# Row maxima ahead of attention placed a little sooner behind DVE by the clock of the program

## The chip, the cores and the metric

The kernel runs on one core of a Trainium2 chip. The metric is the device time of one execution in microseconds; of the kernel before, three runs took 1078.60, 1079.80 and 1075.82 us, with a median of 1078.6 us. The engines are named as in the profile: PE multiplies matrices (PEld is its weight load, which overlaps with the multiplication), DVE and POOL do elementwise work and reductions, ACT does activations and copies, and SP, ACT and POOL issue DMAs. PE writes into PSUM, which has eight banks here (`bk`, 128 partitions x 8 banks x 512 floats).

## The reference

One input x of 2048 tokens by 448 features goes through two branches, and a gate per token mixes them.

```python
qkv = (x @ wqkv).reshape(B, S, 3, H, Dh)          # H = 16 heads, Dh = 28
scores = einsum("bhqd,bhkd->bhqk", q, k) * (Dh ** -0.5)
p = softmax(scores, axis=-1)
a = einsum("bhqk,bhkd->bhqd", p, v) ... @ wo      # branch a: attention
y = layernorm(x)
h = gelu(y @ w1 + b1)                             # 448 -> 1792
b = h @ w2 + b2                                   # branch b: an MLP, 1792 -> 448
g = sigmoid((x * gate_w).sum(-1))
out = g * a + (1 - g) * b
```

The softmax needs, for each head and each query, the largest score over the 2048 keys. The kernel finds it ahead of the attention by computing the scores once more in a cheaper form, and that work is what the change touches.

## The kernel before

**Tiling.** The 2048 tokens are four chunks of 512. The 16 heads are four groups of four, and a group's heads sit in four bands of 32 partitions, so that four matmuls with 28 to 32 contraction rows can work side by side, one in each band of PE's rows. A matmul of the projections or of the MLP is cut into such bands too ("strips"): each strip works through its quarter of the contraction and hands the accumulating bank to the next strip. Values that need more than one pass of the fast float format are split in a high and a low part (`xh`/`xl`, `yh`/`yl`, `w2h`/`w2l`, `hh`/`hl`, `khi`/`klo`).

**Stages.** First come the projections `QK` (query and key, written to DRAM as `qk`) and `Val` (values). Then, per chunk, come 14 `Up` tiles (448 to 1792, weights `w1f`) and 4 `Down` tiles (1792 to 448). All these are pieces of the class `Strips`. Then comes attention, in "turns": a turn computes scores for 5, 6 or 7 units (a unit is 128 keys x 512 queries of one head, three matmuls of line 1179 into one bank), takes their exponentials on ACT (line 1183), and multiplies earlier exponentials with the values (line 1192, a batch is the four heads of one key block). There are 1024 units and 256 batches.

**Row maxima.** There are also 1024 steps of a row maximum. A step (`RowMax.one`, lines 212 and 214) is one matmul of 128 queries x 512 keys (`qd`, `kd`) into a bank and one DVE reduction of that bank to 128 numbers (`mx`). During `Strips` two banks, 6 and 7, serve the steps in turn, so that a step's matmul cannot start before the reduction of the step before last has read the same bank. When a block of 64 steps is complete, DVE reduces it further and transposes it (`close`), SP stores it in DRAM, and the attention loads it as an extra row of the queries.

**What sets the order of PE's instructions.** The order is written out ahead by `Strips.run`, which keeps a clock of its own for each of the four strips and for DVE, ACT and POOL, all from constants in the code. A strip whose clock is lowest is asked first for a row maximum (`Strips.rowmax`), and if it has none, for the next matmul of a piece. If neither can be had, its clock moves on by 0.1 us. A row maximum is given only when its bank's entry in the table `rm` is not later than the strip's clock. That entry is set to the planned end of the bank's reduction plus a pause; a reduction is planned with 0.65 us (`RM`). The clocks decide nothing on the chip. There, engines go through their instructions in the order written, and wait on semaphores.

**What is left over goes into attention.** Steps that `Strips.run` has not placed by its end are placed by `lone` inside the turns of the attention. A turn of 5 units has room for three of them, a turn of 6 for two. `turn_of` makes a turn of 5 as long as more steps are left than the coming turns of 6 could take:

```python
size = 5 if owed and owed > 2 * ((left - 104) // 6) + 6 * sixes[0] else 6
```

Here `owed` is the number of steps left and `left` the number of units left. Turns of 7 come only when no step is left.

Of the kernel before, what the change touches and what calls it, by code (L numbers as in the profile page):

```python
# [35 lines left out]
def kernel(ctx: ExitStack, tc: tile.TileContext, xt, wqk, wv, wo, xk, w1, b1, w2, b2,  # L36
# [367 lines left out]
    class Strips:  # L404
# [92 lines left out]
        def rowmax(self, s, now):  # L497
            if now < self.hot[s] or not rowmax.ready(s):
                return False
            if rowmax.cnt[s] > 5 + min(rowmax.cnt):  # L500
                return False
            b = min(self.rm, key=lambda b: self.rm[b])
            if self.rm[b] > now:
                return False
            ends = rowmax.one(s, bk[:, b])
            self.t[s] = now + 0.232
            self.use("dve", now + 0.45, RM)
            self.rm[b] = self.dve + 0.1
            for kind, n, j in ends:
                if kind == "q":  # L510
                    self.at(now + 6.0, lambda n=n, j=j: rowmax.load_q(n, j))
                elif kind == "k":
                    def load(n=n, j=j):
                        rowmax.load_k(n, j)
                        self.hot[j] = self.get(self.clock + 0.6, 224) + 1.0

                    self.at(now + 1.5, load)
                    self.hot[j] = 1e9
                else:
                    self.at(now + 0.5, lambda n=n: rowmax.close(n), dve=0.45)  # L520
                    self.at(now + 3.0, lambda n=n: rowmax.store(n))
            return True
# [678 lines left out]
    while b < UNITS // 4:  # L1201
# [13 lines left out]
        while 4 * b + 4 <= before and quota:  # L1215
# [7 lines left out]
            b, begun_half = b + 1, False  # L1223
# [59 lines left out]
```

## Time and profile before

The profiled execution took 1078.01 us, with a span of 1076.2 us from its first to its last instruction and a granted TensorE clock of 1.000. It is 0.6 us shorter than the median of the runs.

| what | value |
|---|---|
| median of three runs | 1078.6 us |
| profiled execution / its span | 1078.01 / 1076.2 us |
| row maximum: reduction on DVE (line 214) | x1024, 673.8 us, mean 688 ns |
| row maximum: matmul on PE (line 212) | x1024, 449.4 us busy, mean 440 ns |
| exponentials on ACT (line 1183) | x381, 481.0 us, mean 1316 ns |
| first matmul with `w1f` (start of the MLP) | 125.2 us |
| first score matmul of attention (line 1179) | 450.0 us |

Times count from the start of the span. A busy time of PE is a union of overlapping matmuls, each of which shows about 0.4 us although several run side by side in the four bands, so PE looks full nearly throughout. The busy times of PEld, DVE and ACT say more of what is full in a stage. A row of the timeline gives the start, the time covered, the engine, the line, the operation with its tiles, and how many instructions are merged in it. In brackets stand the idle time of the engine before it and what ended that.

### The profile page before, as it was taken

How to read it: one execution, taken by the hardware profiler on the slowest of the kernel's cores; microseconds unless marked ns; L12 is line 12 of the kernel's file. 1: busy time of each engine (PE TensorE's matmuls, PEld its weight loads, DVE VectorE, ACT ScalarE, POOL GpSimd, SP SyncE). 2: the span in 40 equal slices, each digit the busy share in tenths (PEclk: the TensorE clock that was granted, in tenths of full speed). 3: DMA queues.
4: the chain of work that ended last, by engine and by line, in shares of the span. 5: the costliest groups of instructions: out<-in, count | busy, mean ns of one | idle time of the engine just before them, and what ended most of it. 6: DMA issues, size and time to landing. Idle time of an engine off the chain costs nothing.

```text
span 1076.2 us, 31074 instructions
## 1 busy us (share of the span) xinstructions
PE 1065.3 (99%) x13442; PEld 725.8 (67%) x13442; DVE 740.3 (69%) x1201; ACT 633.2 (59%) x654; POOL 367.5 (34%) x388
## 2 busy tenths in 40 slices
PE   9999999999999999999999999999999999999997
PEld 7999999999999999844444444444444444464555
DVE  4899898999999999876767655676764444422102
ACT  5234364033133033288788788778888888857671
POOL 4565578336244037341001101300110315444431
PEclk9999999999999999999999999999999999999999
DMA  7696433312100104230000001210001201011111
GB/s 252 198 285 196 173 105 95 96 46 61 46 7 7 46 14 116 90 80 18 24 12 27 16 24 46 78 42 6 26 25 27 68 23 55 25 59 31 62 49 66
DMA packets 47785, 73.20 MB, mean 68 GB/s; under 512 B 13840, under 2 KB 28816, under 8 KB 46848
## 3 DMA queue, kind: packets, MB, share of 16 engines
q1 hardware_dynamic: 33888, 39.11, 12.0%
q0 software_dynamic: 5120, 16.89, 5.7%
q10 hardware_dynamic: 8640, 15.21, 3.9%
q8 instruction: 105, 1.72, 0.6%
q14 instruction: 32, 0.26, 0.1%
HBM read 51.75 MB, written 19.31 MB: 66 GB/s over the span
## 4 chain that ended last, share of the span: by engine, by line
PE 97%; ACT 1%; issue 1%; DMA 0%; DVE 0%; DVEq 0%; SPq 0%; ACTq 0%
PE bk L488 35%; PE bk L1192 22%; PE bk L1179 19%; PE bk L212 15%; PE bk L1004 1%; ACT p L1183 1%; PE bk L1005 1%; PE bk L1006 1%; PE bk L920 1%; DMA first<-in_xt 0%; PE bk L948 0%; DVE acc L1011 0%; PE bk L905 0%; PE bk L1079 0%; PE bk L1073 0%
## 5 line engine op out<-in xcount | busy, mean ns | idle before, releaser
L214 DVE TENSOR_REDUCE mx<-bk 128x1 f32<-128x512 f32 x1024 | 673.8, 688 | 215.8 <-PE bk L212 173.3
L1183 ACT ACTIVATE p<-bk 128x1536 f32<-128x1536 f32 (+1 forms) x381 | 481.0, 1316 | 122.5 <-PE bk L1179 122.5
L212 PE MATMUL bk<-kd,qd 28*128 28x512 f32 x1024 | 449.4, 440 | 0.1
L212 PEld LDWEIGHTS bk<-kd,qd 28*128 28x128 f32 x1024 | 186.0, 182 | 176.6 <-DVE mx L214 117.2
L488 PE MATMUL bk<-yh,w1f 32*128 32x512 f32 x1568 | 191.6, 393 | 0.0
L488 PE MATMUL bk<-yl,w1f 32*128 32x512 f32 x784 | 166.6, 391 | 0.0
L488 PEld LDWEIGHTS bk<-yh,w1f 32*128 32x128 f32 x1568 | 154.7, 183 | 1.1
L488 PE MATMUL bk<-w2h,hh 32*128 32x448 f32 x896 | 145.6, 367 | 0.2 <-issue 0.2
L488 PE MATMUL bk<-w2l,hh 32*128 32x448 f32 x896 | 144.5, 363 | 0.0
L1192 PE MATMUL bk<-p,va 128*32 128x512 f32 (+1 forms) x1136 | 130.0, 559 | 0.0
L1192 PE MATMUL bk<-p,vb 128*32 128x512 f32 (+1 forms) x1184 | 129.4, 542 | 0.0
L363 POOL TENSOR_TENSOR hl<-h,hh 128x512 fp32r<-128x512 f32 x56 | 72.5, 1307 | 135.0 <-ACT hh L356 111.7
L840 POOL CAST yh<-yl 128x512 fp32r<-128x512 f32 x16 | 9.8, 611 | 314.7 <-DMA yl<-qk 188.0
L488 PEld LDWEIGHTS bk<-yl,w1f 32*128 32x128 f32 x784 | 106.0, 183 | 0.1
L488 PEld LDWEIGHTS bk<-w2h,hh 32*128 32x128 f32 x896 | 103.1, 183 | 0.9 <-issue 0.6
L488 PEld LDWEIGHTS bk<-w2l,hh 32*128 32x128 f32 x896 | 103.1, 183 | 0.3
L1179 PE MATMUL bk<-yh,ka 29*128 29x512 f32 x512 | 100.6, 483 | 0.4 <-ACT p L1183 0.4
L1179 PE MATMUL bk<-yh,kb 29*128 29x512 f32 x512 | 95.9, 480 | 1.6 <-ACT p L1183 1.6
L488 PE MATMUL bk<-w2h,hl 32*128 32x448 f32 x896 | 93.5, 362 | 0.0
L1179 PE MATMUL bk<-yh,la 28*128 28x512 f32 x512 | 82.9, 393 | 0.0
L488 PEld LDWEIGHTS bk<-w2h,hl 32*128 32x128 f32 x896 | 82.2, 183 | 0.3
L1179 PE MATMUL bk<-yl,ka 28*128 28x512 f32 x512 | 81.8, 407 | 0.0
(142 smaller groups left out, 1528.5 us busy)
## 6 DMA issues: line engine op xcount, KB each, us to landing
qk<-qo ACTq DMA_DIRECT2D x28, 256.0 KB
raw<-in_xt SPq DMA_DIRECT2D x17, 256.0 KB
vs<-vt ACTq DMA_DIRECT2D x16, 256.0 KB
rc<-rls SPq DMA_DIRECT2D x60, 64.0 KB
bxr<-in_xk POOLq DMA_DIRECT2D x8, 448.0 KB, 5.9
acc<-gbs SPq DMA_DIRECT2D x16, 224.0 KB
out_y<-acc SPq DMA_DIRECT2D x16, 224.0 KB
qd<-qk SPq DMA_DIRECT2D x60, 56.0 KB
```

The lines of the kernel that those rows point to most:

```text
L212: nc.tensor.matmul(ps, self.qd[n % 2][r, i * P:(i + 1) * P], self.kd[r, k * 512:(k + 1) * 512], start=True, stop=True)
L214: nc.vector.reduce_max(self.mx[n % 2][:, j, i, k:k + 1], ps, axis=AX)
L363: nc.gpsimd.tensor_sub(hl[f], h, hh[f].bitcast(F32))
L488: mm = nc.tensor.matmul(bk[:, x.bank, :n], a, b, start=x.first, stop=(len(x.rem) == 1 and m == len(ops) - 1), skip_group_check=True)
L840: nc.gpsimd.tensor_copy(h, l.bitcast(F32))
L920: nc.tensor.matmul(bk[:, b], w, v, start=(i == 0), stop=(i == len(ops) - 1), skip_group_check=True)
L1004: nc.tensor.matmul(po, h, woh[:, g], start=(g == 0), stop=False, skip_group_check=True)
L1005: nc.tensor.matmul(po, h, wol[:, g], start=False, stop=False, skip_group_check=True)
L1006: nc.tensor.matmul(po, l, woh[:, g], start=False, stop=(g == NG - 1), skip_group_check=True)
L1179: nc.tensor.matmul(bk[:, place(i)], w[r, ks], q[r], start=(p == 0), stop=(p == 2), skip_group_check=True)
L1183: nc.scalar.activation(t[:, :count], bk[:, b:b + count], AF.Exp, scale=SCALE)
L1192: nc.tensor.matmul(bk[32 * j:32 * j + 32, 7, sl], vg[n // NC][:, k, 32 * j:32 * j + 32], prob[4 * b + j][:, sl], start=(k == 0), stop=(k = ...
```

## The change

One constant in `Strips.rowmax` becomes smaller: the pause between the planned end of a bank's reduction and the moment from which that bank may be given to the next row maximum.

```diff
@@ Strips.rowmax
             ends = rowmax.one(s, bk[:, b])
             self.t[s] = now + 0.232
             self.use("dve", now + 0.45, RM)
-            self.rm[b] = self.dve + 0.1
+            self.rm[b] = self.dve + 0.05
             for kind, n, j in ends:
```

No instruction's work changes, and no tile, bank, load or semaphore is added or removed. What changes is the order of the matmuls on PE from the first stage on, with what follows from it on DVE, ACT, POOL and SP, and how many row maxima stand ahead of the attention. Counted in PE's order, 6762 strip matmuls of line 488 stand ahead of the first score matmul in both kernels. Of the row maxima (line 212) 116 stand ahead of the first matmul with `w1f` in both; ahead of the first score matmul stand 578 before and 571 now, so that 446 before and 453 now are left to the attention. The attention had 124 turns of 5 units, 59 of 6, 7 of 7, one of 1 and a last one of none. Now it has 133 of 5, 51 of 6, 7 of 7, one of 4 and a last one of none: 193 turns instead of 192.

The first place is DVE's order around the end of the strips and the start of attention. It begins behind the third of the three gate instructions (lines 849 to 851, issued when the last `Up` tile is done), and ends at the first copy of an attention result (line 1027). `mx` are row maxima; lines 229 and 230 close a block. The kernel before:

```order
L214 TENSOR_REDUCE mx_154<-bk 128x1 x41
L214 TENSOR_REDUCE mx_155<-bk 128x1 x4
L214 TENSOR_REDUCE mx_154<-bk 128x1 x4
L214 TENSOR_REDUCE mx_155<-bk 128x1
L214 TENSOR_REDUCE mx_154<-bk 128x1
L214 TENSOR_REDUCE mx_155<-bk 128x1 x3
L229 TENSOR_REDUCE mf_156<-mx_154 128x16
L230 STREAM_TRANSPOSE mt_158<-mf_156 128x32
L214 TENSOR_REDUCE mx_155<-bk 128x1 x33
L1027 COPY ob<-bk 128x256
```

The changed kernel at the same place on DVE:

```order
L214 TENSOR_REDUCE mx_154<-bk 128x1 x46
L214 TENSOR_REDUCE mx_155<-bk 128x1
L214 TENSOR_REDUCE mx_154<-bk 128x1 x2
L214 TENSOR_REDUCE mx_155<-bk 128x1 x4
L214 TENSOR_REDUCE mx_154<-bk 128x1
L214 TENSOR_REDUCE mx_155<-bk 128x1
L214 TENSOR_REDUCE mx_154<-bk 128x1
L214 TENSOR_REDUCE mx_155<-bk 128x1 x4
L229 TENSOR_REDUCE mf_156<-mx_154 128x16
L230 STREAM_TRANSPOSE mt_158<-mf_156 128x32
L214 TENSOR_REDUCE mx_155<-bk 128x1 x24
L1027 COPY ob<-bk 128x256
```

In this stretch stood 87 row maxima and now stand 84; ahead of the gates stood 530 and now stand 526. So the first attention result stands behind 617 row maxima before and behind 610 now.

The second place is PE's order in the 120th turn of the attention, between two products with the values (line 1192, `p` are exponentials, `va` the values). `ka`, `la`, `yh` and `yl` are the high and low parts of keys and queries. The kernel before:

```order
L212 MATMUL bk<-kd,qd_152 128x512
L1179 MATMUL bk<-yh,ka 128x512 x3
L1179 MATMUL bk<-yh,la 128x512 x3
L1179 MATMUL bk<-yl,ka 128x512 x3
L1179 MATMUL bk<-yh,ka 128x512 x3
L1179 MATMUL bk<-yh,la 128x512 x3
L212 MATMUL bk<-kd,qd_152 128x512
L1179 MATMUL bk<-yl,ka 128x512 x3
L1192 MATMUL bk<-p_13552,va 32x512 x2
L1192 MATMUL bk<-p_13575,va 32x512 x2
```

The changed kernel in its 120th turn on PE:

```order
L212 MATMUL bk<-kd,qd_152 128x512
L1179 MATMUL bk<-yh,ka 128x512 x3
L1179 MATMUL bk<-yh,la 128x512 x3
L1179 MATMUL bk<-yl,ka 128x512 x3
L212 MATMUL bk<-kd,qd_152 128x512
L1179 MATMUL bk<-yh,ka 128x512 x2
L1179 MATMUL bk<-yh,la 128x512 x2
L212 MATMUL bk<-kd,qd_152 128x512
L1179 MATMUL bk<-yl,ka 128x512 x2
L1192 MATMUL bk<-p_13537,va 32x512 x2
L1192 MATMUL bk<-p_13561,va 32x512 x2
```

The turn had 6 units (18 score matmuls) and two row maxima; now it has 5 units (15 score matmuls) and three. The turns of 5 go on for nine more turns before the turns of 6 begin.

## The prediction

> **What bounds the kernel now.** I read the page's first part, then the busy time by stage, then the row maxima by stage, then the waits and the timeline inside the stages. The page:
>
> ```profile
> span 1076.2 us, 31074 instructions
> PE 1065.3 (99%) x13442; PEld 725.8 (67%) x13442; DVE 740.3 (69%) x1201; ACT 633.2 (59%) x654; POOL 367.5 (34%) x388
> ...
> L214 DVE TENSOR_REDUCE mx<-bk 128x1 f32<-128x512 f32 x1024 | 673.8, 688 | 215.8 <-PE bk L212 173.3
> ```
>
> PE covers 99% of the span, but its rows overlap (four bands at once), so this share doesn't tell where it is full. The weight loads and DVE, neither full overall, change from stage to stage. The row maxima's reductions are the costliest group, 688 ns on the mean. I cut the span at the start of the MLP, the start of the attention, a point five turns into the first turns of 6, and near the last turns (columns: stretch, its length, then busy time and instructions of each engine, TensorE clock, DMA share, GB/s):
>
> ```profile
> 0.00:124.50 124.50, 121.87 (x1857) 112.52 (x1857) 99.40 (x176) 49.29 (x98) 72.46 (x118) 1.00 0.71 226
> 124.50:450.00 325.50, 325.30 (x5537) 311.44 (x5534) 315.28 (x494) 100.53 (x167) 150.31 (x132) 1.00 0.20 59
> 450.00:813.80 363.80, 363.49 (x3482) 168.67 (x3481) 241.51 (x391) 295.05 (x249) 51.85 (x53) 1.00 0.13 36
> 813.80:984.80 171.00, 169.95 (x1840) 81.27 (x1836) 72.55 (x117) 140.18 (x103) 60.57 (x58) 1.00 0.15 44
> 984.80:1076.20 91.40, 84.71 (x743) 51.88 (x739) 11.59 (x25) 48.17 (x40) 32.29 (x29) 1.00 0.16 54
> ```
>
> In the MLP stage, 325.5 us long, PEld is busy for 311.44 us and DVE for 315.28 us, both nearly all of it. In the stretch of the turns of 5 (450.0 to 813.8) DVE falls to 66% and ACT rises to 81%; in the turns of 6 DVE is at 42%. The clock is 1.00 in all of these. The same stretches with the row maxima's reductions alone:
>
> ```profile
> 0.00:124.50 124.50, 73.26 (x114) 1.00 0.71 226
> 124.50:450.00 325.50, 303.00 (x466) 1.00 0.20 59
> ```
>
> In the MLP stage 466 reductions take 303.00 us, 0.650 us each where they follow one another, so the DVE of that stage is the row maxima and 12.3 us of other work, with 325.5 - 315.28 = 10.2 us idle. Who waits for whom between 100 and 450 us:
>
> ```profile
> DVE mx L214 <- PE bk L212: 7.3, 11, 1.6
> PEld bk L212 <- DVE mx L214: 1.0, 4, 0.3
> ```
>
> DVE waited 7.3 us for a row maximum's matmul, and PE's loads stood idle 1.0 us for a reduction. So PE and DVE are both close to full, and neither holds the other for long. Whether a matmul is ready just in time is seen in the last microseconds of the stage:
>
> ```profile
> 445.67 3.90 DVE L214 TENSOR_REDUCE mx<-bk 128x1 f32<-128x512 f32 x6
> 446.42 0.18 PEld L212 LDWEIGHTS bk<-kd,qd 28*128 28x128 f32 x1
> 447.06 0.18 PEld L212 LDWEIGHTS bk<-kd,qd 28*128 28x128 f32 x1
> 447.70 0.18 PEld L212 LDWEIGHTS bk<-kd,qd 28*128 28x128 f32 x1
> 448.35 0.18 PEld L212 LDWEIGHTS bk<-kd,qd 28*128 28x128 f32 x1
> ```
>
> Six reductions in 3.90 us end every 0.65 us, at about 446.32, 446.97, 447.62 and 448.27. The matmuls that take the freed banks begin their loads at 446.42, 447.06, 447.70 and 448.35, that is 0.08 to 0.10 us later: what the chip does lies near the 0.1 us that the program planned. This slack is what the change halves.
>
> **The change part by part.** *The strips up to 125 us.* Where the MLP begins is seen in the rows of its weights (least, median and largest ns, first and last start):
>
> ```profile
> L488 PE MATMUL bk<-yh,w1f x1568: 382/389/500, 125.2 to 410.2; 32*128 32x512 f32 x196
> ```
>
> Both orders have 116 row maxima and the same pieces ahead of the first `w1f` matmul at 125.2 us, so I put nothing there. In that stretch DVE is busy for 99.40 of 124.5 us, and PE covers 121.87, so a row maximum a little sooner or later there finds room.
>
> *The strips from 125 to 450 us.* The same 6762 strip matmuls end with 571 row maxima placed and not with 578. What 7 fewer are worth depends on what fills the stage. If it is PE's matmul slots, the stage has 5537 PE instructions in 325.5 us, 0.059 us each, and 7 fewer give 0.4 us. If it is DVE, they give 7 x 0.650 = 4.6 us. DVE's full 96.9% and its reductions end to end are the nearer row, since the smaller number of row maxima for the same strip work says that the strips of the new order stand idle less often beside DVE, and it is DVE that paces them. On top of it the earlier release can close some of DVE's idle 10.2 us: 455 row maxima released 0.05 us sooner would be 22.8 us if each passed it on, but there are only 10.2 us to gain, and the 0.65 us rhythm above has none. I take an eighth, 1.3 us. So the strips end 4.6 + 1.3 = 5.9 us sooner; the ends are 0.4 us and 4.6 + 10.2 = 14.8 us.
>
> *What waits at the end of the strips.* Attention's first keys and queries must be split by POOL before it begins. The last of that in the kernel before, and the first score matmul:
>
> ```profile
> 434.42 1.29 POOL L825 TENSOR_TENSOR la<-la,ka 128x512 fp32r<-128x512 f32 x1
> 436.01 0.60 POOL L828 DMA_DIRECT2D ka<-ones  x1 [0.29 <-POOL la L825]
> 450.01 0.50 PE L1179 MATMUL bk<-yh,ka 29*128 29x512 f32 x3
> ```
>
> The split ends at 435.7 us and the load of the last key row is issued by 436.6 us, over 13 us ahead of the first score matmul at 450.0. It hangs on the last `Up` tile, which has moved in the order as well (526 row maxima ahead of the gates and not 530: about 4 x 0.650 = 2.6 us sooner). If the strips end 5.9 us sooner, the cover shrinks by some 3 us and stays at about 10 us. If it were gone, each microsecond of lateness would go to the end time.
>
> *The attention.* It gets 7 more row maxima, 9 more turns of 5, 8 fewer of 6, and a turn of 4 for one of 1. Turns of 5, with one batch of values (eight rows, since each matmul shows twice) and with two:
>
> ```profile
> 540.74 0.49 PE L212 MATMUL bk<-kd,qd 28*128 28x512 f32 x1
> 542.46 1.06 PE L1192 MATMUL bk<-p,va 128*32 128x512 f32 x8
> 543.46 0.49 PE L212 MATMUL bk<-kd,qd 28*128 28x512 f32 x1
> 545.16 1.92 PE L1192 MATMUL bk<-p,va 128*32 128x512 f32 x16
> 547.02 0.50 PE L212 MATMUL bk<-kd,qd 28*128 28x512 f32 x1
> ```
>
> From the row maximum that opens a turn to the first value matmul are 1.72 and 1.70 us; the turns last 2.72 and 3.56 us, so that a batch costs 0.84 us more and a turn without a batch 1.88 us. A turn of 6 with a batch and a half:
>
> ```profile
> 823.32 0.50 PE L212 MATMUL bk<-kd,qd 28*128 28x512 f32 x1
> 825.04 1.50 PE L1192 MATMUL bk<-p,va 128*32 128x256 f32 x16
> 826.47 0.50 PE L212 MATMUL bk<-kd,qd 28*128 28x512 f32 x1
> ```
>
> Its scores take 825.04 - 823.32 = 1.72 us, as in a turn of 5, and the turn lasts 3.15 = 1.88 + 1.5 x 0.84 us. So a turn has the same price with 5 units and three row maxima as with 6 and two, and the 256 batches are the same in all. The attention grows by its one more turn, 1.88 us. The turn of 1 unit:
>
> ```profile
> 1052.24 0.49 PE L1179 MATMUL bk<-yh,kb 29*128 29x512 f32 x1
> 1053.12 1.50 PE L1192 MATMUL bk<-p,vb 128*32 128x256 f32 x16
> ```
>
> It takes 0.88 us to its values and a turn of 4 has two halves as one of 5 has, 1.72 us: 0.84 us more. The attention costs 1.88 + 0.84 = 2.7 us; its ends are 1.5 us (the last turn's scores hidden beside ACT) and 4 us (one more turn's wait for the last exponentials). Seven more reductions on a DVE that is busy 66% there cost nothing: the batches cover them, and without that cover 7 x 0.69 = 4.8 us would come in.
>
> *The added risk.* With half the pause, a reduction that runs late makes PE wait at the head of its queue, and all four strips behind it. Nothing in the trace prices this. From below it is nothing, as the 1.0 us of idle loads says; from above each of 455 row maxima waits the whole 0.05 us, 22.8 us. I take nothing, being nearest to the row, since a wait once taken moves all later matmuls back and gives the next ones their slack again.
>
> *The sum.* -5.9 + 2.7 = -3.2 us on the profiled execution's 1078.0 us (span 1076.2 and 1.8 us around it) gives 1074.8 us. The median of the runs is 0.6 us above that execution, within their spread of 4 us; I say 1075.0 us.
>
> **The rivals.** *A: PE is what fills the strips.* For it speaks PEld with 311.44 of 325.5 us. Then 7 fewer row maxima save 0.4 us, the attention adds 2.7 us, and the time is 1078.0 + 2.3 = 1080.3 us. Against it: PE instructions per us differ within the strips (1857 in 124.5 us at first, 14.9 per us, and 17.0 in the MLP stage), so PE had room. The Trainium skill's "Perfetto Trace Analysis", section Identifying the Most-Contended Engine, judges TensorE by the busy share of its weight loads and other engines by their occupancy, and calls the highest the bound: by it the stage would go to DVE, 96.9% against 95.7%, too narrow a lead to settle it, and where weight loads bind the sum would be rival A's.
>
> *B: the bank is not free in time.* DVE's reductions run 0.02 us or more later than the order supposes, and each of the 455 matmuls holds PE. For it: the slack seen is 0.08 to 0.10 us, and 0.03 to 0.05 us would be left. Against it: the loads' idle 1.0 us. At 0.03 us each it costs 13.7 us, and the time is 1074.8 + 13.7 = 1088.5 us, slower than before. It decides from 3.2 us on against the gain, 0.007 us for each row maximum, and reaches 0.5% slower from 0.019 us.
>
> *C: DVE's gaps close.* Half of the idle 10.2 us goes as well: -4.6 - 5.1 + 2.7 = -7.0, 1071.0 us. For it: the pause is part of every bank's round. Against it: the 0.65 us rhythm shows none of the gap, so the gaps stand where no strip had a row maximum to give.
>
> *D: the change doesn't do what it says.* Row maxima would come sooner only relative to DVE; in the order fewer of them stand ahead of the attention, not more. This is already in the sum, as its attention term.
>
> **How the numbers follow.** Forecast 0.60, A 0.14, B 0.10, C 0.16. What a measurement can tell from no change is about 0.5%, 5.4 us: faster means below 1073.2 us, slower above 1084.0 us. C is all faster, and of the forecast's own range, 1072 to 1077 us, I give about a sixth to below 1073.2: 0.16 + 0.10 = 0.26. B is slower, 0.10. The rest, with A, is the same, 0.64. The range reaches from C's 1071.0 to a little above A, 1081 us, and leaves out B and the far ends of the unknown costs.
>
> **What would show it.** In the changed kernel's profile the first score matmul (line 1179) should stand near 444 us and not 450.0, with 571 row maxima ahead of it, about 0.65 us apart where they run end to end. From there to the end should be about 629 us (626.2 before), with turns of 5 still 2.7 us with one batch. PE's loads waiting for `mx` between 100 and 450 us should stay under a few microseconds; tens of them would be rival B. A first score matmul at 449.6 us would be A. The prediction would be wrong if attention started late for its keys, or if a stretch of the new order made a strip, ACT or POOL wait where nothing waits now.

## The result and the profile after

The changed kernel takes 1080.8 us (median of 22 runs, 1075.1 to 1084.5) against 1077.4 us (22 runs, 1075.8 to 1080.4) for the kernel before. The ratio is 1.0024 with a 95% interval of 1.0017 to 1.0032: about 2.6 us slower (3.4 us by the medians), where 3 us faster was forecast. Its runs spread wider than those of the kernel before, and four of the 22 lie at 1075 to 1077 us. That spread turned out to matter.

The page of the changed kernel, and its busy time by the same stages as before:

```profile
span 1079.5 us, 30962 instructions
PE 1066.3 (99%) x13386; PEld 722.7 (67%) x13386; DVE 743.0 (69%) x1201; ACT 634.7 (59%) x657; POOL 368.9 (34%) x388
```

```profile
124.50:450.00 325.50, 323.13 (x5553) 307.94 (x5549) 314.58 (x488) 101.06 (x167) 151.61 (x133) 0.99 0.20 60
450.00:813.80 363.80, 363.21 (x3448) 168.67 (x3447) 244.51 (x396) 293.53 (x250) 51.97 (x53) 1.00 0.13 37
984.80:1079.50 94.70, 87.28 (x769) 52.84 (x761) 11.58 (x25) 51.34 (x42) 34.10 (x30) 1.00 0.16 53
```

The DVE of the MLP stage is as full as before, 314.58 of 325.5 us, but PE covers 2.2 us less of that stage, and its clock is at 0.99. The stage begins and ends at these rows (the `w1f` matmuls with the first and last start, and the first score matmuls):

```profile
L488 PE MATMUL bk<-yh,w1f x1568: 382/389/623, 126.1 to 412.1; 32*128 32x512 f32 x196
450.01 0.50 PE L1179 MATMUL bk<-yh,ka 29*128 29x512 f32 x2
```

The attention starts at 450.01 us, as before, and not near 444 us: with 7 fewer row maxima ahead of it, it comes no sooner. (The MLP stage began 0.9 us later than before and was 0.9 us shorter.) From there to the end are 1079.5 - 450.0 = 629.5 us, 3.3 us more than before, which is all of the loss in the span. Who held PE between 100 and 450 us:

```profile
PEld bk L212 <- DVE mx L214: 4.0, 7, 2.8
PE bk L212 <- DVE mx L214: 2.4, 1, 2.4
```

Before, PE's idle time for reductions was 1.0 us with 0.3 us as the longest. Now there is a single wait of 2.8 us. (This list counts only time in which no weight load runs at all.) It stands in PE's timeline here:

```profile
167.16 0.39 PE L488 MATMUL bk<-yh,w1f 32*128 32x512 f32 x1
169.92 0.50 PE L212 MATMUL bk<-kd,qd 28*128 28x512 f32 x1 [2.37 <-DVE mx L214]
```

DVE and POOL at that place, where line 153 is the split `w2l = w2 - w2h` of a block of MLP weights (odd blocks on DVE, even ones on POOL), and line 363 the split of `h`:

```profile
161.55 1.65 DVE L153 TENSOR_TENSOR w2l<-raw,w2h 128x448 fp32r<-128x448 f32 x1
163.12 1.96 DVE L214 TENSOR_REDUCE mx<-bk 128x1 f32<-128x512 f32 x3
164.99 4.27 DVE L153 TENSOR_TENSOR w2l<-raw,w2h 128x448 fp32r<-128x448 f32 x1
169.19 2.61 DVE L214 TENSOR_REDUCE mx<-bk 128x1 f32<-128x512 f32 x4
171.71 0.61 DVE L153 TENSOR_TENSOR w2l<-raw,w2h 128x448 fp32r<-128x448 f32 x1
```

```profile
164.38 0.73 POOL L160 DMA_DIRECT2D lnr<-lns  x1
165.13 2.56 POOL L363 TENSOR_TENSOR hl<-h,hh 128x512 fp32r<-128x512 f32 x2
167.63 1.14 POOL L153 TENSOR_TENSOR w2l<-raw,w2h 128x448 fp32r<-128x448 f32 x1
```

The DVE split at 164.99 takes 4.27 us, and the same form 0.61 us at 171.71. POOL works without a gap from 165.13 to 168.77 (two splits of `h`, one of `w2l`), and the DVE split ends 0.49 us after that. Behind it on DVE stand the row maxima, and behind the banks of those stands PE, whose queue holds all four strips.

A row of POOL splits without a gap isn't enough for that. The kernel before had one too, DVE and then POOL:

```profile
144.54 1.72 DVE L153 TENSOR_TENSOR w2l<-raw,w2h 128x448 fp32r<-128x448 f32 x1
144.47 4.20 POOL L363 TENSOR_TENSOR hl<-h,hh 128x512 fp32r<-128x512 f32 x3
```

There the DVE split ended 0.48 us after the first of POOL's three, and POOL's second took 1.70 us where the other two took 1.30: the two engines took turns. At 164.99 DVE was passed over three times. Six of the twelve profiles below have such a long hold (3.11 to 4.80 us), and in all six POOL's splits follow right behind its issue of the DMA of line 160, as here at 164.38. In the kernel before no DVE split began beside those, but for one 0.08 us before the last of them ended. Whether that issue is the reason isn't shown.

And when PE goes on, it is slow for a while (columns as above):

```profile
167.00:170.00 3.00, 0.63 (x12) 0.20 (x5) 3.00 (x3) 0.00 (x0) 1.77 (x2) 1.00 0.51 132
170.00:172.00 2.00, 2.00 (x30) 1.98 (x34) 2.00 (x4) 0.00 (x0) 0.00 (x0) 0.76 0.70 236
172.00:174.00 2.00, 2.00 (x26) 2.00 (x24) 1.61 (x3) 0.83 (x2) 0.00 (x0) 0.50 0.35 112
174.00:176.00 2.00, 2.00 (x35) 1.98 (x29) 0.30 (x2) 1.55 (x3) 1.29 (x1) 0.89 0.13 46
```

PE covers 0.63 of 3 us, and then the granted clock is 0.76, 0.50 and 0.89 for six microseconds. In the kernel before the whole stage has a mean of 1.00.

### The profile page after: what moved, and what is told of

Read it like the earlier page. It is cut to its first block, busy times and chain, and to the rows that moved or that the text cites. A ratio compares the mean times of both kernels' runs of the same rounds, so it can differ in the third digit from the quotient of the medians.

```text
span 1079.5 us, 30962 instructions
## 1 busy us (share of the span) xinstructions
PE 1066.3 (99%) x13386; PEld 722.7 (67%) x13386; DVE 743.0 (69%) x1201; ACT 634.7 (59%) x657; POOL 368.9 (34%) x388
## 3 DMA queue, kind: packets, MB, share of 16 engines
q1 hardware_dynamic: 33888, 39.11, 12.3%
q8 instruction: 105, 1.72, 0.6%
## 4 chain that ended last, share of the span: by engine, by line
PE 96%; ACT 2%; issue 1%; DVE 1%; DMA 0%; SPq 0%; ACTq 0%; DVEq 0%
PE bk L488 35%; PE bk L1192 22%; PE bk L1179 19%; PE bk L212 15%; PE bk L1004 1%; ACT p L1183 1%; PE bk L1006 1%; PE bk L1005 1%; PE bk L920 1%; DVE w2l L153 0%; DMA first<-in_xt 0%; DVE acc L1011 0%; PE bk L905 0%; PE bk L948 0%; DVE mx L214 0%
## 5 line engine op out<-in xcount | busy, mean ns | idle before, releaser
L1183 ACT ACTIVATE p<-bk 128x1536 f32<-128x1536 f32 (+2 forms) x384 | 481.2, 1307 | 125.1 <-PE bk L1179 125.1
L488 PE MATMUL bk<-yh,w1f 32*128 32x512 f32 x1568 | 189.2, 393 | 0.0
L488 PE MATMUL bk<-yl,w1f 32*128 32x512 f32 x784 | 163.7, 393 | 0.0
L488 PEld LDWEIGHTS bk<-yh,w1f 32*128 32x128 f32 x1568 | 151.3, 184 | 2.0 <-ACT h L355 0.3
L488 PE MATMUL bk<-w2h,hh 32*128 32x448 f32 x896 | 140.2, 369 | 0.0
L488 PE MATMUL bk<-w2l,hh 32*128 32x448 f32 x896 | 138.6, 366 | 0.0
L488 PE MATMUL bk<-w2h,hl 32*128 32x448 f32 x896 | 89.2, 363 | 0.0
L355 ACT ACTIVATE h<-bk,b1s 128x512 f32<-128x512 f32 x56 | 38.4, 685 | 72.0 <-PE bk L488 67.5
## 6 DMA issues: line engine op xcount, KB each, us to landing
bxr<-in_xk POOLq DMA_DIRECT2D x8, 448.0 KB, 6.3
```

The costliest lines, as they stand in the source:

```text
L355: nc.scalar.activation(h, bk[:, self.bank], AF.Gelu_apprx_tanh, bias=b1s[:, f:f + 1])
L488: mm = nc.tensor.matmul(bk[:, x.bank, :n], a, b, start=x.first, stop=(len(x.rem) == 1 and m == len(ops) - 1), skip_group_check=True)
L1183: nc.scalar.activation(t[:, :count], bk[:, b:b + count], AF.Exp, scale=SCALE)
```

## The experiments

In this table each row is one profiled execution. The MLP stage is the time from the first `w1f` matmul to the first score matmul, the attention from there to the end of the span. Medians and ratios are those of the timed runs; the kernel before had medians of 1077.3 to 1077.6 us beside them. DVE's busy and idle time add up to the MLP stage.

| kernel | MLP stage | DVE busy + idle in it | attention | longest DVE split | median | ratio to before (95%) |
|---|---|---|---|---|---|---|
| before | 324.8 | 314.6 + 10.2 | 626.2 | 1.72 | 1077.4 | |
| changed | 323.9 | 312.9 + 10.9 | 629.5 | 4.27 | 1080.8 | 1.0024 (1.0017 to 1.0032) |
| changed, again | 318.8 | 308.9 + 10.0 | 631.1 | 0.69 | 1080.1 | 1.0028 (1.0017 to 1.0040) |
| changed, block 11 on POOL | 319.6 | 310.4 + 9.2 | 630.8 | 1.63 | 1077.8 | 1.0002 (0.9992 to 1.0011) |
| before, block 11 on POOL | 324.9 | 315.0 + 9.8 | 626.4 | 1.74 | 1077.8 | 1.0003 (0.9994 to 1.0012) |
| before, capped at 569 | 323.4 | 309.0 + 14.4 | 629.6 | 1.73 | 1079.5 | 1.0015 (1.0005 to 1.0024) |
| changed, stores by POOL | 323.5 | 313.5 + 10.0 | 629.5 | 4.24 | 1080.6 | 1.0027 (1.0014 to 1.0040) |
| changed, both | 319.7 | 309.5 + 10.2 | 629.1 | 1.65 | 1076.0 | 0.9985 (0.9976 to 0.9993) |
| pause 0.02 | 330.2 | 319.1 + 11.1 | 627.2 | 3.81 | 1084.3 | 1.0058 (1.0044 to 1.0072) |
| pause 0.03 | 330.6 | 315.9 + 14.7 | 628.0 | 3.45 | 1082.1 | 1.0038 (1.0025 to 1.0052) |
| pause 0.03, block 11 on POOL | 326.9 | 315.2 + 11.6 | 628.1 | 3.11 | 1081.5 | 1.0040 (1.0025 to 1.0055) |
| pause 0.02, block 11 on POOL | 334.0 | 320.1 + 13.9 | 627.1 | 4.80 | 1086.2 | 1.0083 (1.0063 to 1.0102) |

**The changed kernel once more.** No edit.

> The changed kernel as it is, for a second profile of the same order. Theory 1 (SBUF path): the DVE split of w2l (line 153) that took 4.27 us beside POOL's back-to-back work in the first profile is long here too, at about 165 us, PE stands near 2 us behind it, and the median is 1080 to 1081 us against 1077.4 us before. Theory 2 (late banks, rival B): no such split need be long; PE's waits for mx are many and short, spread over the strips, and add up to the same 3 us. If neither shows, the first profile was an accident of one execution, and this profile should have its first score matmul near 445 us.

Measured: 1080.1 us (1077.8 to 1083.7), so the loss is there again. But the execution that was profiled was a good one, 1077.8 us, the fastest of its ten. It shows what the order does when the split isn't held. DVE, then POOL, at the same place:

```profile
161.53 0.61 DVE L153 TENSOR_TENSOR w2l<-raw,w2h 128x448 fp32r<-128x448 f32 x1
164.71 0.61 DVE L153 TENSOR_TENSOR w2l<-raw,w2h 128x448 fp32r<-128x448 f32 x1
```

```profile
164.36 0.73 POOL L160 DMA_DIRECT2D lnr<-lns  x1
165.11 2.62 POOL L363 TENSOR_TENSOR hl<-h,hh 128x512 fp32r<-128x512 f32 x2
```

Here the split of block 9 took 0.61 us and not 1.65 (and POOL's split beside it 1.62 us and not 1.15; in both profiles the two began within 0.01 us of each other). So that of block 11 came up at 164.71 and not at 164.99. It began while POOL was still issuing a DMA, 0.40 us ahead of POOL's splits and not 0.14 us, and wasn't held. A quarter of a microsecond stands between 0.61 and 4.27 us. And the strips then end where the forecast had put them:

```profile
L488 PE MATMUL bk<-yh,w1f x1568: 382/389/502, 126.1 to 407.0; 32*128 32x512 f32 x196
444.89 0.50 PE L1179 MATMUL bk<-yh,ka 29*128 29x512 f32 x2
445.83 0.49 PE L1179 MATMUL bk<-yh,ka 29*128 29x512 f32 x1 [0.43 <-ACT gb L398]
```

444.89 - 126.1 = 318.8 us for the stage, 6.0 us less than before. So the profile of the result and this one are the two faces of one order. That also answers the last part of the expectation: whether the split is held changes from one execution to the next. Two of the three profiles of the changed order with this split on DVE have it (4.27 and 4.24 us), and the timed runs suggest that most executions do.

**The held split taken off DVE.** In the changed kernel, and as a control in the kernel before:

```diff
-        (nc.vector if f % 2 else nc.gpsimd).tensor_sub(w2l[f], r, w2h[f].bitcast(F32))
+        (nc.vector if f % 2 and f != 11 else nc.gpsimd).tensor_sub(w2l[f], r, w2h[f].bitcast(F32))
```

> The changed kernel with the one split that was long (w2l of block 11) given to POOL and not to DVE; the order on PE and ACT is the same. Theory 1: no row maximum is held behind it, PE doesn't stand near 167 us, its clock stays at 1.00 there, the first score matmul comes 3 to 4.5 us sooner (445.5 to 447 us) and the time is 1076 to 1078 us. Theory 2: nothing of this changes, 1080 to 1081 us, since all banks are handed out as before.

> The kernel before with the same one split on POOL, as a control. Its split of block 11 took 0.62 us, so theory 1 expects no gain: 1077 to 1078 us, ratio 0.999 to 1.001. If the time falls by 2 us or more here as well, the split costs DVE something in any order and the run e2 would say nothing on the change.

Measured: 1077.8 us in the changed kernel, 2.3 to 3.0 us less than its two medians, and 1077.8 us in the kernel before, where it changes nothing (ratio 1.0003). The edit touches none of the program's clocks, so PE's order is that of the changed kernel. The strips end early again:

```profile
L488 PE MATMUL bk<-yh,w1f x1568: 382/389/500, 124.8 to 406.4; 32*128 32x512 f32 x196
444.35 0.50 PE L1179 MATMUL bk<-yh,ka 29*128 29x512 f32 x2
```

So the cost that made the changed kernel slower than before is the DVE split held by POOL, and not the pause: the banks are handed out exactly as in the changed kernel here. All ten runs lie between 1076.3 and 1078.6 us, so the wide spread is gone with it.

**Fewer row maxima alone.** The kernel before, with the last nine left to the attention:

```diff
-            if now < self.hot[s] or not rowmax.ready(s):
+            if now < self.hot[s] or not rowmax.ready(s) or sum(rowmax.cnt) >= 569:
```

> The kernel before with the strips' row maxima capped at 569 and not 578: the last nine are left to the attention, all else in the strips' order is the same up to there, and the attention has 193 turns instead of 192 (131 of 5, 53 of 6, 7 of 7, one of 2). It measures by itself what fewer row maxima ahead of the attention are worth. By the prediction's rule (DVE paces the strips, 0.65 us each) the first score matmul comes 5.9 us sooner, at 444, and the attention is 2.2 us longer, 1073.7 us. If PE's slots fill the strips (rival A) it comes 0.5 to 0.9 us sooner, at 449.2, and the time is 1078.8 us.

Measured: 1079.5 us, 1.6 us more than before by the ratio, near the time of rival A.

```profile
L488 PE MATMUL bk<-yh,w1f x1568: 382/390/504, 124.6 to 409.2; 32*128 32x512 f32 x196
448.00 0.50 PE L1179 MATMUL bk<-yh,ka 29*128 29x512 f32 x3
```

The stage lasts 448.0 - 124.6 = 323.4 us, 1.4 us less for nine row maxima, 0.16 us each. That is far from the prediction's 0.65 us. But the cap took the last nine, so DVE was left without work at the end. The last 5.2 us of the stage:

```profile
442.80:448.00 5.20, 5.20 (x75) 4.38 (x67) 0.03 (x1) 1.24 (x3) 1.67 (x3) 1.00 0.50 158
```

DVE's busy time fell by 5.6 us and its idle time rose by 4.2: there the strips had too much work of their own left to end much sooner. So this run prices a row maximum at the end of the stage, and suggests that PE's own work is close behind DVE's. It doesn't price one in the middle, where the two run in step. The changed order without a held split differs: in its two profiles DVE's busy time fell by 4.2 and 5.7 us (the reductions by 4.3 us in both) and its idle time stayed at 9.2 and 10.0 us, so that the stage shortened with DVE. No run tells whether the 7 row maxima or the new layout of PE's matmuls is the cause of that.

The first turn of the attention took 3.96 us here (3.19 before), and with it the attention grew by 3.4 us; without that wait it grew by 2.6 us for the one more turn, where the expectation had 2.2.

**The stores ahead of the first turn.** In the second profile of the changed kernel the first row of attention above is followed, 0.94 us later, by one that waits for ACT (0.43 us, `gb`). That is ACT, copying the four last `Down` tiles out of their banks (line 398). The kernel before and then the changed kernel, the first and the last of these copies and the store behind the first:

```profile
446.79 0.54 ACT L398 ACTIVATE gb<-bk 128x448 f32<-128x448 f32 x1 [33.23 <-PE bk L488]
447.36 0.33 ACTq L401 DMA_DIRECT2D gbs<-gb  x1
449.79 0.54 ACT L398 ACTIVATE h<-bk 128x448 f32<-128x448 f32 x1 [0.46 <-ACT h L398]
```

```profile
448.34 0.55 ACT L398 ACTIVATE h<-bk 128x448 f32<-128x448 f32 x1 [32.92 <-PE bk L488]
448.92 0.33 ACTq L401 DMA_DIRECT2D gbs<-h  x1
451.30 0.54 ACT L398 ACTIVATE gb<-bk 128x448 f32<-128x448 f32 x1 [0.40 <-ACT gb L398]
```

Each copy of 0.54 us is followed by the issue of its store, 0.33 us, and a gap, so that one takes 1.0 us. Before, the first copy began 3.2 us ahead of the first score matmul at 450.01, now 1.7 us, since the four strips end nearly together. The first turn lasted 3.19 us before, and 4.37, 5.64 and 5.29 us in the changed order's first three profiles. In the two long ones the clock falls as well; the second profile's start of attention:

```profile
446.00:448.00 2.00, 2.00 (x14) 1.13 (x15) 0.00 (x0) 1.42 (x2) 1.69 (x2) 0.92 0.87 245
448.00:450.00 2.00, 2.00 (x6) 1.49 (x5) 0.00 (x0) 1.49 (x2) 0.88 (x2) 0.50 0.77 287
450.00:452.00 2.00, 2.00 (x17) 1.08 (x15) 0.68 (x1) 0.19 (x1) 0.81 (x1) 0.72 0.43 137
```

The edit issues the last chunk's four stores from POOL:

```diff
-            nc.scalar.dma_start(gbs[self.c * TPC + self.i], gb)
+            (nc.gpsimd if self.c == NC - 1 else nc.scalar).dma_start(gbs[self.c * TPC + self.i], gb)
```

> The changed kernel, with the last chunk's four stores of gbs issued by POOL and not by ACT. In the changed order the four last Down tiles end within a microsecond, and their copies run on ACT at 1.0 us each, 0.54 us of copy and the rest store issue and gap; the first turn of the attention waits for the banks. If that is what makes the first turn 4.4 to 5.6 us long (3.19 us in the kernel before), it falls to 3.2 to 3.6 us and the time by 1 to 2 us: 1078.5 to 1079.5 us, still with the long split in most runs. If the turn is long for another reason (keys late from POOL), it stays at 4.4 us or more and the time at 1080 to 1081 us.

> The changed kernel with both: the split of block 11 on POOL, and the last stores issued by POOL. If the two costs are separate and are all that the prediction had left out, what remains is its own sum: 1077.8 us of the split's run less 1 to 2 us, 1075.8 to 1076.8 us, ratio 0.998 to 0.9995. If the stores only move the wait, 1077.8 us.

Measured: alone, the first turn falls to 3.19 us as expected, but the median stays at 1080.6 us. The profile says where the gain went. Counted from the first score matmul, its exponentials (line 1183) run 1.2 us ahead of those of the changed kernel's first profile behind the first turn. Then they lose 0.25 to 0.3 us at each of six places, 32 turns apart, and the attention is 629.5 us as there. The profile with both edits loses at the same places, the two other profiles of the changed order at none of them. What makes these places longer isn't shown. Together with the moved split the time is 1076.0 us, 1.9 us less than with the split alone, and 0.15% less than the kernel before, with an interval that excludes no change (0.9976 to 0.9993). Its rows:

```profile
span 1073.3 us, 30964 instructions
L488 PE MATMUL bk<-yh,w1f x1568: 382/389/500, 124.5 to 406.3; 32*128 32x512 f32 x196
444.21 0.75 PE L1179 MATMUL bk<-yh,ka 29*128 29x512 f32 x4
442.56 0.98 ACT L398 ACTIVATE h<-bk 128x448 f32<-128x448 f32 x2 [32.89 <-PE bk L488]
443.43 0.99 ACT L398 ACTIVATE gb<-bk 128x448 f32<-128x448 f32 x2
```

ACT's copies now follow each other in pairs of 0.98 us, the first turn takes 3.19 us and the clock stays up. The attention is 629.1 us, 2.8 us more than before. It loses time at the six places too. But against the split alone, where the first turn's wait came with the fall of the clock, it gains 1.7 us in the attention (629.1 and 630.8 us).

**Shorter pauses.** The same line of the change, with 0.02 and 0.03 in place of 0.05, and then with block 11's split on POOL:

> The kernel before with a pause of 0.02 us, shorter than the change's. Its order has 582 row maxima ahead of the attention and the same turns as before (124 of 5, 59 of 6, 7 of 7, one of 1), so the attention stays at 626 us. Rival B (banks handed out too early make PE wait): more than the changed kernel loses, 3 us and up, 1081 to 1090 us, with PE's waits for mx up from 1 us to many. If the pause itself costs nothing and only the order counts: 1075 to 1080 us, with those waits at 1 to 2 us except where a split on DVE runs long.

> The kernel before with a pause of 0.03 us: 576 row maxima ahead of the attention, and again the same turns as before. Rival B: slower than before, as above. If the pause itself costs nothing, the attention is 626 us and the strips end at 446 to 450 us: 1074.5 to 1078 us, and a new order that keeps the turns can gain where the changed one lost.

> The pause of 0.03 us with the split of block 11 on POOL. In the profile of the pause of 0.03 us that split took 3.45 us on DVE, and PE stood 1.74 us behind it. If held splits make up the loss of the shorter pauses, the time falls by 2.5 to 4 us, from 1082.1 to 1078 to 1079.5 us. If late banks (rival B) make it up, it stays at 1081 us or more.

> The pause of 0.02 us with the split of block 11 on POOL; it took 3.81 us there, and PE stood 2.26 us behind it. Held splits: 1084.3 us falls to 1080 to 1081.5 us, and what stays above the kernel before (3 to 4 us) belongs to the order and to PE's many short waits for mx. Late banks: 1083.5 us or more.

Measured: 1084.3 and 1082.1 us, and 1086.2 and 1081.5 us with block 11 moved. The attention stayed near 627 to 628 us (626.2 before); most of the loss is in the MLP stage, 330 us and not 325. Both have a held split, 3.81 and 3.45 us. But moving that one split helped little or not at all (0.6 us less, and 1.9 us more): with it gone another is held, the longest of all in the last of these kernels. Its DVE and POOL:

```profile
167.09 4.80 DVE L153 TENSOR_TENSOR w2l<-raw,w2h 128x448 fp32r<-128x448 f32 x1
```

```profile
165.41 1.31 POOL L363 TENSOR_TENSOR hl<-h,hh 128x512 fp32r<-128x512 f32 x1
166.67 1.16 POOL L153 TENSOR_TENSOR w2l<-raw,w2h 128x448 fp32r<-128x448 f32 x1
170.13 1.27 POOL L363 TENSOR_TENSOR hl<-h,hh 128x512 fp32r<-128x512 f32 x1
```

POOL has five splits end to end from 165.41 to 171.40, the DVE split of another block comes up at 167.09 and ends at 171.89, 0.49 us after POOL's last. Again the five follow an issue of line 160. So the holding belongs to two engines that split at the same time, and block 11 was only the one that the changed order brought into it. Late banks are there too. PE's idle time for reductions between 30 and 440 us, with a pause of 0.02 us:

```profile
PEld bk L212 <- DVE mx L214: 6.0, 20, 2.3
```

20 waits where the kernel before had 5 in the same stretch, and 6.0 us where it had 1.1, of which 2.3 us are the held split. So rival B exists at 0.02 us with 2 to 3 us more of visible waits than before; at the change's 0.05 us, in the second profile, there are 6 waits with 1.2 us, nearly as before. How the rest of the shorter pauses' loss divides between held splits, waits for hand-offs between strips (one of 1.3 to 1.8 us in each of the four) and late banks is left open. In the table DVE's idle time has grown as well, to 11.1 to 14.7 us.

## Why the prediction was wrong

**The strips up to 125 us.** Right: `w1f` begins at 126.1, 126.1 and 124.8 us in three profiles of the changed order and at 125.2 us before. The difference is there before the first strip matmul (18.3, 18.3 and 16.6 us against 16.8 us) and belongs to the execution.

**The strips from 125 to 450 us, -5.9 us.** Right in size for an execution without a held split: -6.0 us in the changed kernel's second profile and -5.2 us with the split moved. Its main part, 4.6 us for seven fewer reductions, is there as DVE time: the reductions of the stage fell by 4.3 us. The 1.3 us from DVE's gaps were 0.3 and 1.0 us. But the rule behind it, 0.65 us for each row maximum because DVE paces the strips, is only half borne out: nine fewer at the end of the stage gave 1.4 us. What the seven are worth where they are missing in the changed order stays open, and part of the agreement may be luck.

**The slack that the change was to halve.** The prediction read 0.08 to 0.10 us between a reduction's end and the next load, and took this for the planned pause of 0.1 us. One reduction of the kernel before at that place, and one of the changed kernel with its load:

```profile
445.67 0.69 DVE L214 TENSOR_REDUCE mx<-bk 128x1 f32<-128x512 f32 x1
```

```profile
443.56 0.69 DVE L214 TENSOR_REDUCE mx<-bk 128x1 f32<-128x512 f32 x1
444.30 0.18 PEld L212 LDWEIGHTS bk<-kd,qd 28*128 28x128 f32 x1
```

A row lasts 0.69 us though the next begins 0.65 us after it. So the reductions end at 446.36 and 444.25, and the loads at 446.42 and 444.30 follow 0.05 to 0.06 us later with either pause. Over the whole stage the median is 0.05 us, before and now, and with pauses of 0.03 and 0.02 us as well. So on the chip there was no planned pause to be shortened: in all these orders most loads of a row maximum begin just behind the end of a reduction. Only the order changed.

**The added risk, taken as nothing.** This is the step that failed and turned the sign. The prediction looked for lateness in the banks only, one reduction at a time, and found 1.0 us of waits. What else stands in DVE's queue was put down as "12.3 us of other work", taken to stay as it was. In it stood splits of 1.72, 1.33 and 1.63 us beside others of 0.62 us, in the profile of before: they were already held then by POOL, only briefly. The changed order put one into the POOL splits behind the issue of line 160. It cost DVE 3.7 us, PE a wait of 2.4 us with a low clock behind it, and the stage 5.1 us between the two profiles of the same order (323.9 and 318.8 us); the other work of DVE in the stage is 14.6 us in the one and 10.9 us in the other. The split's removal (-2.3 to -3.0 us in the median) shows that the timed runs pay for it too. The prediction's closing sentence named the case, a stretch of the new order in which an engine waits where nothing waited, but the sum gave it no price and the chances had no place for it: rival B, many late banks at 1088 us, is another mechanism.

**What waits at the end of the strips.** POOL's splits of the keys were early enough, as said. That ACT must empty four banks at 1.0 us each wasn't asked. It costs 1.2 us at the first turn (4.37 us against 3.19 us), and up to 2.5 us where the clock falls too.

**The attention, +2.7 us.** Right for its own terms: 2.8 us where the first turn is 3.19 us long (both edits), and 2.1 to 3.2 us in the other profiles of the change at 0.05 us, less what their first turn is longer. A turn of 5 costs what a turn of 6 costs, and one more turn is what counts. With the first turn's wait it was 3.3 to 4.9 us. With both edits the change gains 1.6 us by the ratio, half of the 3.2 us of the sum; the six places that lose time with the moved stores cost about 1.6 us.

**The rivals.** A (1080.3 us) gives the measured time with another mechanism: without a held split the strips didn't stay long for PE's slots, as the second profile shows, though A's price of a row maximum is the nearer one at the end of the stage. B's mechanism, many short waits, didn't come at 0.05 us and did at 0.02 us. C's did not show: DVE's gaps stayed at 9.2 to 10.9 us. The Trainium skill's "Perfetto Trace Analysis", section Identifying the Most-Contended Engine, calls the engine of highest occupancy the bottleneck, here DVE by a narrow lead. The traces agree so far as the stage changed with DVE's busy time (308.9 to 314.6 us); the run with nine fewer suggests how close PE was behind it.

## What to carry to other kernels

When a constant re-orders a whole stage, count its work, but then walk the new order of each in-order queue for the rare long instructions in it: what is behind them, and which other engine can hold them. Spread in the durations of one form (0.61 to 1.72 us here) in the profile of before is the sign that something else already holds it; if a busy queue stands behind, price the worst case. A run that takes work away at the end of a stage doesn't price that work in the middle. Runs that spread wider than those of the kernel before are worth a second profile: here the two outcomes of one order lay side by side and showed gain and loss apart.

## What the runs showed of the hardware

A DVE subtraction of two SBUF tensors (128x448) took 0.61 us alone and up to 4.80 us beside POOL; the six long ones ended 0.48 to 0.50 us after the last of POOL's subtractions that followed each other without a gap. Reductions out of PSUM stayed at 0.65 to 0.69 us beside the same POOL work. That the two engines share a path to SBUF is what the Trainium skill's "SBUF — State Buffer", section Who interferes with whom, states for DVE instructions with two SBUF inputs. The trace agrees (4.27 us against 0.61 us). It adds that the waiting one is mostly let in behind one POOL instruction (1.72 us at 144.54 in the kernel before), but in these six cases was passed over by all that were left of the row, twice even though its own row in the trace began 0.13 and 0.14 us ahead of the first of them. Which of the two happens isn't explained here.

PE's clock fell to 0.50 after a single wait of 2.4 us in an otherwise full stretch, and again at the start of attention after a wait of 0.4 us in a thin one. In the changed kernel's first profile the second of these didn't happen, with the same wait, and with a pause of 0.02 us the clock stayed at 1.00 behind a wait of 1.9 us (at 171 us). The Trainium skill's "TensorE: Matmul & The Clock Gate", Part 1, says that the clock falls after an idle window of about 3.4 us; the waits that did it here were shorter, and no run here shows the window.
